# An opening in another order: C loaded by heads, the table load ahead of ScalarE's DMA issues, two weight pieces decoded in other steps (Mamba-2 SSD, then a hard-swish MLP, one core)

## The chip, the cores and the metric

The kernel runs on one core of a Trainium2 chip. The metric is the device time of one execution in microseconds (us). Three runs of the kernel before took 360.72, 358.92 and 364.13 us, median 360.72 us.

## The reference, cut to what matters

Batch is 4, heads 8, sequence 768, head size 32, state size 16; the MLP has width 256 and inner width 2048. Its weights come as float64.

```python
log_a = np.log(np.clip(a, 1e-06, 1.0))
for c in range(nc):                       # chunks of the sequence
    cum = np.cumsum(la, axis=-1)
    L = np.exp(cum[:, :, :, None] - cum[:, :, None, :]) * causal
    M = np.einsum('bhin,bhjn->bhij', Cc, Bc) * L
    y = np.einsum('bhij,bhjd->bhid', M, xc) + np.einsum('bhin,bhnd->bhid', Cc, state) * np.exp(cum)[..., None]
    state = decay_full * state + np.sum(Bx, axis=2)     # Bx: B times x, decayed to the chunk's end
...
h = x @ w_in                              # x: y with the heads joined, 3072 x 256
g = h * np.clip(h + 3.0, 0.0, 6.0) / 6.0
out = g @ w_out
```

## The kernel before, in words

The sequence is cut into six chunks of 128 positions; a chunk holds all four batches, so 512 tokens. For each chunk the kernel forms the decays L, multiplies them with C times B (`scores`, `multiply`), applies them to x (`mix`), keeps the result turned as yT (`keep`), and runs the MLP on it. A chunk is worked on in two halves of 64 positions; the second half starts from a middle state `mid`.

The schedule is written by hand: each engine executes its instructions in the order in which the program lists them, and the framework adds only waits. A tile with a tag in a pool of one buffer is given to the next tile of that tag when the last reader of the earlier one is done, wherever that reader stands in the program. PSUM banks f0 to f3, y0, y1 and two called o are passed on in this way.

**Loads.** SyncE's queue (SP) issues the loads of `a`, C, x and most weight pieces; ScalarE's queue (ACT) issues the first weight piece (`load_w(0)`) and chunk 0's B, and then loads the activation table (line 146). For chunk 0 (and chunks 3 to 5, where B comes so too) C comes through `pairs_first` (lines 96 to 103): eight DMAs of 32 KB, one for each batch b and head parity h. Each fills all 128 partitions: its source is four heads by 32 groups of positions by 64 numbers, which lie together as 256 bytes.

**Weights.** A float64 weight is decoded on the core from its two 32-bit words. Four pieces of w_in and four of w_out, 1 MB each as loaded, go through a generator `decode(i)` (lines 187 to 237), and `weights(i, n)` carries out the next n of its steps. The operations of one piece are: words (L198, ScalarE, copies the top 16 bits), masks (L215 and L217, VectorE, exponent and sign), upper (L201, VectorE, the upper significand), lower (L205, VectorE, adds the low word), two ramps on the exponent, above (L221) and below (L223, both ScalarE), sign (L228, VectorE) and product (L236, VectorE, writes w_in or w_out). Three buffers hold raw pieces.

**Opening.** For chunk 0, TensorE builds exponent differences in PSUM (`diff`), ScalarE exponentiates them (`diff_exp`, L365), B is turned by TensorE and copied by ScalarE (`turn_b`, bT), C is turned by VectorE (`turn_squares`, L465, csT) and split by head parity (`part_heads`, L472, cT). `first_eto` makes the decay from the chunk's start (e_ps in bank f0, L376), by which GpSimd fades csT (`fade`, L478). `scores(0)` multiplies C and B (cb in f0 to f3, L522) and forms the state's terms (`into_state`, L534). `multiply(0)` multiplies cb into L on VectorE (four times L563), while ScalarE copies out `adds` (`take`, L550) and `mid` (L558). `turn_cum` turns the sums of the later chunks into c_ps, in bank f1, and `by_token` (L319, VectorE) reads it. `mix(0)` multiplies L with x (L588) in two halves, u = 0 and u = 1, each followed by `from_state` (L500); its second half writes bank f1 (tile y2). `keep(0)` has four copies on ScalarE (L602). `busy(n)` is n dummy products of the identity with itself, whose result nobody reads.

Then TensorE runs the first product of the MLP for chunk 0, `mlp_in(0, f)` for f = 0 to 15 (L610); four f use one piece of w_in. Its results go through `ramp` (L688, ScalarE) and `times_ramp` (L693, VectorE), which frees the bank for f + 4. Pieces 2 to 5 are decoded between them (the `weave`), and pieces 6 and 7 after them; the second product, `first_out` (L707), follows and takes a piece of w_out in each of its four rounds.

Of the kernel before, what the change touches and what calls it, by code (L numbers as in the profile page):

```python
# [8 lines left out]
FP32 = mybir.dt.float32  # L9
# [11 lines left out]
def kernel(  # L21
# [63 lines left out]
    def load_bc(c):  # L85

        sl = slice(c * P, (c + 1) * P)

        def tokens_first(src, queue=nc.sync, **where):
            t = loads.tile([P, NB * NH, N], FP32, **where)
            queue.dma_start(out=t, in_=src[:, :, sl, :].rearrange("b h s n -> s (b h) n"))
            return t

        def pairs_first(src):
            t = loads.tile([P, 2, NB, 4, N], FP32, name="pairs", tag="bc")
            for b in range(NB):
                for h in range(2):
                    nc.sync.dma_start(  # L100
                        out=t[:, h, b].rearrange("s a n -> s (a n)"),
                        in_=src[b, h:NH:2, sl, :].rearrange("h (s a) n -> h s (a n)", a=4))
            return t

        if 0 < c < TURN:
            bcs[c] = [tokens_first(C, name="C", tag="bc")]
        Bs[c] = tokens_first(B, nc.scalar if c == 0 else nc.sync, name="B")
        if c == 0:
            bcs[c] = [pairs_first(C), Bs[c]]
        elif c < TURN:  # L110
            bcs[c].append(Bs[c])
        else:
            bcs[c] = [pairs_first(C), pairs_first(B)]
# [14 lines left out]
    def load_w(i, queue=nc.sync):  # L128
# [10 lines left out]
        queue.dma_start(out=dst, in_=src)  # L139
        raws[i] = raw  # L140

    load_w(0, nc.scalar)
    load_bc(0)
    load_x(0)
    load_w(1)
    nc.scalar.preload_act_table_set("natural_log_exp_and_others")


    ident = const.tile([P, P], FP32, name="ident")
# [37 lines left out]
    def decode(i):  # L187

        n = NK * FP * P
        top = raws[i].bitcast(U16).rearrange("p (n w) -> p n w", w=4)[:, :, 3]
        lo, hi = (raws[i].rearrange("p (n w) -> p n w", w=2)[:, :, w] for w in range(2))
        s = att.tile([P, n], U16, name="ws")
        e = att.tile([P, n], U16, name="we")
        m = att.tile([P, n], U32, name="wm")
        nc.scalar.copy(out=s, in_=top)  # L198

        def significand():  # L200
            nc.vector.tensor_scalar(  # L201
                out=m, in0=hi, scalar1=0xFFFFF, scalar2=0x100000,
                op0=ALU.bitwise_and, op1=ALU.bitwise_or)
            yield
            nc.vector.scalar_tensor_tensor(  # L205
                out=m.bitcast(FP32), in0=lo, scalar=2.0 ** -32, in1=m, op0=ALU.mult,
                op1=ALU.add)
            yield

        parts_m = significand()  # L210
        if i == 0:
            next(parts_m)
            next(parts_m)
        yield
        nc.vector.tensor_scalar(  # L215
            out=e, in0=s, scalar1=0x7FF0, scalar2=None, op0=ALU.bitwise_and)
        nc.vector.tensor_scalar(  # L217
            out=s, in0=s, scalar1=0x8000, scalar2=None, op0=ALU.bitwise_and)
        next(parts_m, None)
        yield  # L220
        nc.scalar.activation(e.bitcast(BF16), e, AF.Relu, bias=bias_hi, scale=-8.0)  # L221
        yield
        nc.scalar.activation(e, e.bitcast(BF16), AF.Relu, bias=bias_lo, scale=-1.0)  # L223
        next(parts_m, None)
        if i and i + NRAW < 2 * NP:
            load_w(i + NRAW)
        yield
        nc.vector.tensor_tensor(out=e, in0=e, in1=s, op=ALU.bitwise_or)  # L228
        m, e = m.bitcast(FP32), e.bitcast(BF16)
        if i < NP:  # L230
            dst = w_in[:, :, i * FP * P:(i + 1) * FP * P]
            m, e = (t.rearrange("p (k f) -> p k f", k=NK) for t in (m, e))
        else:
            dst = w_out[:, (i - NP) * FP:(i - NP + 1) * FP, :]
            m, e = (t.rearrange("p (k f) -> p k f", k=FP) for t in (m, e))
        nc.vector.scalar_tensor_tensor(  # L236
            out=dst, in0=m, scalar=2.0 ** -20, in1=e, op0=ALU.mult, op1=ALU.mult)

    pick = const.tile([P, G], BF16, name="pick")
    less = const.tile([P, G], BF16, name="less")
# [258 lines left out]
                    rhs=csT[pair, b, HALF[a]], start=(a == 0 and b == 0), stop=True,  # L502
                    tile_position=(32 * q, d0), skip_group_check=True)

    def scores(c):

        bT, cT, _ = bTs[c]
        cbs[c] = [ps.tile([P, NB, 2, HT], FP32, name="cb", tag=f"f{q}") for q in range(NQ)]
        both = [ps_y.tile([P, 2, NB, HT], FP32, name=f"y{u}", tag=f"y{u}") for u in range(2)]
        ys[c] = {(0, u): both[u][:, 0] for u in range(2)}
        sps[c] = [both[a if c else 1 - a][:, 1] for a in range(2)]
        if c:
            from_state(c, 0)
        for b in range(NB):
            for a, rows in enumerate(HALF):
                for q in range(NQ):  # L520
                    pair = slice(32 * q, 32 * q + 32)
                    nc.tensor.matmul(  # L522
                        out=cbs[c][q][rows, b], lhsT=bT[pair, b, rows],
                        rhs=cT[pair, b, :, rows], start=(b == 0), stop=True,
                        tile_position=(32 * q, a * HT), skip_group_check=True)
        into_state(c, 0, 1)

    def into_state(c, *halves):
# [19 lines left out]
    def take(c):  # L548
        adds[c] = att.tile([P, NB, 2 * D], FP32, name="adds", bufs=1)
        nc.scalar.copy(out=adds[c], in_=sps[c][1])  # L550

    def multiply(c):

        take(c)
        mids[c] = mid = att.tile([P, NB, 2 * D], FP32, name="mid", bufs=1)
        if c == 0:
            for t in range(2):
                nc.scalar.activation(  # L558
                    mid[:, :, t * D:(t + 1) * D], sps[c][0][:, :, t * D:(t + 1) * D], AF.Copy,
                    scale=parity[:, t:t + 1])  # L560
        for q in range(NQ):
            hs = slice(2 * q, 2 * q + 2)
            nc.vector.tensor_tensor(  # L563
                out=Ls[c][:, :, hs], in0=Ls[c][:, :, hs], in1=cbs[c][q], op=ALU.mult)
            if c and q == 1:
                new_state(mid, sps[c][0], tmps[c])
# [292 lines left out]
        mask_again(0, b)  # L859
    diff(0, 0, 1)  # L860
    diff(0, 2, 3)
    weights(0, 1)
    for b in range(NB):
        diff_exp(0, b)
    first_eto()
    diff(1, 2, 3)
    weights(0, 1)
    for b in range(NB):
        ends(0, b)
    turn_b(0)  # L870
    diff(1, 0, 1)
    weights(0, 1)
    diff_exp(1, 2)
    diff_exp(1, 3)
    turn_squares(bcs[0][0], turned(0)[2])
    part_heads(0)
    fade(0, HALF[1], nc.gpsimd)
    add_up(ends_at[1])
    store_rows()
    load_w(2)  # L880
    weights(0, 1)
    scores(0)
    multiply(0)
    load_w(3)
    c_ps = ps.tile([P, NC, G], FP32, name="c_ps", tag="f1")
    turn_cum(c_ps)
    busy(1, ps.tile([P, NB * P], FP32, name="d", tag="f0"))
    weights(0, 1)
    weights(1, 1)
    by_token(c_ps)  # L890
    mix(0)
    keep(0)
    weights(1, 3)
    renew(0)
    weights(1, 1)
    load_eto(1)
# [138 lines left out]
```

## Time and profile before

| what | us |
|---|---|
| median of three runs | 360.72 |
| the profiled execution, its own time | 359.64 |
| span of its profile (first to last instruction) | 357.9 |
| of the span, before the first L610 matmul | 23.3 |
| TensorE busy, whole span | 347.9 |
| VectorE busy, whole span | 221.9 |
| ScalarE busy, whole span | 177.5 |

All shapes and numbers below come from one profiled execution. A row of the timeline gives start, duration, engine, line, operation, and what it writes from what; in brackets stand the idle time of the engine before it and what ended that. "PEld" is TensorE's loading of the stationary operand, "SPq" an issue on SyncE's queue. A duration is from start to finish; the next instruction of VectorE or ScalarE can start some 0.1 us before an instruction ends, if it does not need its result. TensorE executes a 32-bit matmul as two instructions, so the 32 products of `mlp_in` are 64 matmuls in the profile.

### The profile page before, as it was taken

The numbers are of one execution on the slowest core, as the hardware profiler recorded it, in microseconds if no ns is written. First come the engines' busy times: TensorE is split into PE (matmuls) and PEld (weight loads), VectorE is DVE, ScalarE is ACT, GpSimd is POOL, SyncE is SP. The second block draws the span as 40 slices with busy tenths as digits, with TensorE's granted clock in tenths as the row PEclk, the third lists the DMA queues.
The fourth block names the chain that finished last, engine by engine and source line by source line (L and its number), as shares of the span: only waits on it lengthen the run. The fifth ranks groups of instructions, "written<-read, shape, count | busy, mean of one in ns | idle before, by whom it ended". The sixth has DMA issues, their size and how long they took to land.

```text
span 357.9 us, 9350 instructions
## 1 busy us (share of the span) xinstructions
PE 347.9 (97%) x3936; PEld 300.0 (84%) x3936; DVE 221.9 (62%) x426; ACT 177.5 (50%) x390; POOL 137.9 (39%) x139
## 2 busy tenths in 40 slices
PE   5799999999999999999999999999999999999996
PEld 2554458888888999888999888999888999888996
DVE  6599999975887463686444687434587431588111
ACT  4678887267763730674650575560576010476100
POOL 3300000362599521099522089610068600058700
PEclk9899999999999999999999999999999999999999
DMA  8979969502924061550043560001000000000000
GB/s 166 201 277 185 266 165 127 116 4 84 155 57 60 5 136 58 81 80 2 4 113 82 74 88 2 4 2 35 26 2 1 4 3 31 29 3 0 2 29 31
DMA packets 75482, 24.97 MB, mean 70 GB/s; under 512 B 66032, under 2 KB 71824, under 8 KB 74928
## 3 DMA queue, kind: packets, MB, share of 16 engines
q1 hardware_dynamic: 71056, 23.06, 33.9%
q10 hardware_dynamic: 4384, 1.31, 1.7%
q8 instruction: 31, 0.51, 0.6%
q14 instruction: 11, 0.09, 0.1%
HBM read 21.07 MB, written 3.29 MB: 68 GB/s over the span
## 4 chain that ended last, share of the span: by engine, by line
PE 91%; DVE 3%; DMA 3%; ACT 1%; SPq 1%; issue 0%; DVEq 0%; ACTq 0%
PE ob L766 18%; PE even L652 18%; PE oa L766 18%; PE odd L652 13%; PE o L707 8%; PE h L610 8%; PE y L588 3%; PE y L500 2%; PE cb L522 2%; DMA raw<-in_moe_w_in_dram 2%; DMA pairs<-in_C_dram 1%; PE y L534 1%; SPq L100 1%; DVE odd L681 0%; DVE up L668 0%
## 5 line engine op out<-in xcount | busy, mean ns | idle before, releaser
L752 POOL TENSOR_TENSOR s<-gT 128x512 f32<-128x512 f32 x20 | 26.4, 1318 | 89.7 <-DVE gT L693 89.7
L652 PE MATMUL even<-ts,w_sum 128*128 128x256 f32 x160 | 48.2, 383 | 0.0
L667 ACT COPY even<-odd 128x512 f32<-128x512 f32 x40 | 23.0, 576 | 48.6 <-PE odd L652 46.3
L688 ACT ACTIVATE gT<-odd,half 128x512 f32<-128x512 f32 x40 | 27.5, 688 | 34.9 <-DVE odd L681 34.9
L652 PE MATMUL odd<-yT,w_in 128*128 128x256 f32 x160 | 41.1, 379 | 0.0
L766 PE MATMUL oa<-w_out,gT 128*128 128x128 f32 x320 | 38.9, 277 | 0.0
L766 PEld LDWEIGHTS oa<-w_out,gT 128*128 128x128 f32 x320 | 38.1, 192 | 0.9
L766 PE MATMUL ob<-w_out,s 128*128 128x128 f32 x320 | 37.4, 275 | 0.0
L766 PEld LDWEIGHTS ob<-w_out,s 128*128 128x128 f32 x320 | 36.5, 192 | 0.0
L652 PEld LDWEIGHTS even<-ts,w_sum 128*128 128x128 f32 x160 | 29.9, 190 | 5.3 <-ACT up L674 1.5
L693 DVE SCALAR_TENSOR_TENSOR gT<-gT,odd 128x512 f32<-128x512 f32 x40 | 27.5, 688 | 9.9 <-ACT gT L688 9.9
L652 PEld LDWEIGHTS odd<-yT,w_in 128*128 128x128 f32 x160 | 30.1, 190 | 3.9
L385 ACT ACTIVATE L<-L,cum_n 128x64 f32<-128x64 f32 x128 | 31.1, 339 | 0.0
L766 PE MATMUL ob<-t,gT 128*128 128x128 f32 x240 | 30.3, 279 | 0.0
L688 ACT ACTIVATE gT<-even,half 128x512 f32<-128x512 f32 x40 | 27.8, 695 | 4.4 <-PE even L652 4.4
L693 DVE SCALAR_TENSOR_TENSOR gT<-gT,even 128x512 f32<-128x512 f32 x40 | 27.2, 680 | 4.4 <-ACT gT L688 4.4
L766 PEld LDWEIGHTS ob<-t,gT 128*128 128x128 f32 x240 | 27.9, 192 | 1.2 <-issue 0.5
L707 PE MATMUL o<-w_out,gT 128*128 128x256 f32 x128 | 28.7, 381 | 0.0
L668 DVE COPY up<-odd 128x256 f32<-128x256 f32 x40 | 17.0, 424 | 18.6 <-ACT even L667 17.9
L610 PE MATMUL h<-yT,w_in 128*128 128x512 f32 x64 | 27.7, 594 | 0.0
L707 PEld LDWEIGHTS o<-w_out,gT 128*128 128x128 f32 x128 | 24.1, 190 | 3.7 <-issue 0.5
L563 DVE TENSOR_TENSOR L<-L,cb 128x512 f32<-128x512 f32 x24 | 15.3, 681 | 18.0 <-PE cb L522 15.5
(130 smaller groups left out, 609.8 us busy)
## 6 DMA issues: line engine op xcount, KB each, us to landing
raw<-in_moe_w_out_dram SPq DMA_DIRECT2D x4, 1024.0 KB
L<-cum_d SPq DMA_DIRECT2D x8, 512.0 KB
xt<-in_x_dram SPq DMA_DIRECT2D x6, 512.0 KB
raw<-in_moe_w_in_dram SPq DMA_DIRECT2D x3, 1024.0 KB
out_dram<-res SPq DMA_DIRECT2D x20, 128.0 KB
eto<-cum_e SPq DMA_DIRECT2D x20, 64.0 KB
B<-in_B_dram SPq DMA_DIRECT2D x5, 256.0 KB
raw<-in_moe_w_in_dram ACTq DMA_DIRECT2D x1, 1024.0 KB
```

The source lines that it names most:

```text
L385: nc.scalar.activation(Ls[c][:, b, h], Ls[c][:, b, h], AF.Exp, bias=cum_n[:, c, g:g + 1])
L563: nc.vector.tensor_tensor(out=Ls[c][:, :, hs], in0=Ls[c][:, :, hs], in1=cbs[c][q], op=ALU.mult)
L588: nc.tensor.matmul(out=ys[c][a, u][d0:d0 + D, b], lhsT=xt[rows, b * NH + h], rhs=Ls[c][rows, b, h], start=(b == 0 and a >= min(c, 1)), sto ...
L610: nc.tensor.matmul(out=h.rearrange("p r i -> p (r i)"), lhsT=w_in[:, j, f * P:(f + 1) * P], rhs=yTs[k][:, j].rearrange("p b i -> p (b i)") ...
L652: nc.tensor.matmul(out=bank[:, r], lhsT=lhsT, rhs=rhs, start=start, stop=True, skip_group_check=True)
L667: nc.scalar.copy(out=even, in_=odd[:, 1:2].to_broadcast([P, 2, 2 * P]))
L668: nc.vector.tensor_copy(out=up[:, 1], in_=odd[:, 0])
L688: nc.scalar.activation(gTs[k][:, f], h.rearrange("p r i -> p (r i)"), AF.Relu, bias=half, scale=1.0 / 6.0)
L693: nc.vector.scalar_tensor_tensor(out=g, in0=g, scalar=1.0, in1=h.rearrange("p r i -> p (r i)"), op0=ALU.min, op1=ALU.mult)
L707: nc.tensor.matmul(out=o[:, b % 2], lhsT=gTs[0][:, f, b * P:(b + 1) * P], rhs=w_out[:, f], start=(f == 0 and b % 2 == 0), stop=True, skip_ ...
L752: nc.gpsimd.tensor_tensor(out=o, in0=p_, in1=q_, op=op)
L766: nc.tensor.matmul(out=bank[:, slot], lhsT=lhs[:, j], rhs=rhs[:, j], start=(clear and j == 0), stop=True, skip_group_check=True)
```

## The change

C's (and in chunks 3 to 5 B's) eight loads are divided by head instead of by batch: a load now fills 32 partitions with all four batches of one head. The activation table is loaded before ScalarE's two DMA issues. `decode` is rewritten as named steps with an order for piece 0, one for piece 1, and one for the rest, which is the order that those had. The opening's calls stand in another order: the second running sum and the stores first, `turn_squares` and `part_heads` before the exponentials, `first_eto` after `turn_b`, the dummy product before `scores` and not before `mix`, piece 0's lower step after `multiply`, piece 1's words after `keep`, and `by_token` after `mix`, `keep` and piece 1's upper step. Two things move inside functions: `diff(1, 0, 1)` is called between the score products and `into_state`, and `take` follows the `mid` copies in chunk 0. `load_w(3)` is issued by piece 0's step `more`.

```diff
@@ -95,11 +95,11 @@
 
         def pairs_first(src):
             t = loads.tile([P, 2, NB, 4, N], FP32, name="pairs", tag="bc")
-            for b in range(NB):
+            for q in range(NQ):
                 for h in range(2):
                     nc.sync.dma_start(
-                        out=t[:, h, b].rearrange("s a n -> s (a n)"),
-                        in_=src[b, h:NH:2, sl, :].rearrange("h (s a) n -> h s (a n)", a=4))
+                        out=t[32 * q:32 * q + 32, h].rearrange("s b a n -> s b (a n)"),
+                        in_=src[:, 2 * q + h, sl, :].rearrange("b (s a) n -> s b (a n)", a=4))
             return t
 
         if 0 < c < TURN:
@@ -139,11 +139,11 @@
         queue.dma_start(out=dst, in_=src)
         raws[i] = raw
 
+    nc.scalar.preload_act_table_set("natural_log_exp_and_others")
     load_w(0, nc.scalar)
     load_bc(0)
     load_x(0)
     load_w(1)
-    nc.scalar.preload_act_table_set("natural_log_exp_and_others")
 
 
     ident = const.tile([P, P], FP32, name="ident")
@@ -195,49 +195,59 @@
         s = att.tile([P, n], U16, name="ws")
         e = att.tile([P, n], U16, name="we")
         m = att.tile([P, n], U32, name="wm")
-        nc.scalar.copy(out=s, in_=top)
-
-        def significand():
+
+        def words():
+            nc.scalar.copy(out=s, in_=top)
+
+        def masks():
+            nc.vector.tensor_scalar(
+                out=e, in0=s, scalar1=0x7FF0, scalar2=None, op0=ALU.bitwise_and)
+            nc.vector.tensor_scalar(
+                out=s, in0=s, scalar1=0x8000, scalar2=None, op0=ALU.bitwise_and)
+
+        def upper():
             nc.vector.tensor_scalar(
                 out=m, in0=hi, scalar1=0xFFFFF, scalar2=0x100000,
                 op0=ALU.bitwise_and, op1=ALU.bitwise_or)
-            yield
+
+        def lower():
             nc.vector.scalar_tensor_tensor(
                 out=m.bitcast(FP32), in0=lo, scalar=2.0 ** -32, in1=m, op0=ALU.mult,
                 op1=ALU.add)
+
+        def above():
+            nc.scalar.activation(e.bitcast(BF16), e, AF.Relu, bias=bias_hi, scale=-8.0)
+
+        def below():
+            nc.scalar.activation(e, e.bitcast(BF16), AF.Relu, bias=bias_lo, scale=-1.0)
+
+        def more():
+            if i + NRAW < 2 * NP:
+                load_w(i + NRAW)
+
+        def sign():
+            nc.vector.tensor_tensor(out=e, in0=e, in1=s, op=ALU.bitwise_or)
+
+        def product():
+            m_, e_ = m.bitcast(FP32), e.bitcast(BF16)
+            if i < NP:
+                dst = w_in[:, :, i * FP * P:(i + 1) * FP * P]
+                m_, e_ = (t.rearrange("p (k f) -> p k f", k=NK) for t in (m_, e_))
+            else:
+                dst = w_out[:, (i - NP) * FP:(i - NP + 1) * FP, :]
+                m_, e_ = (t.rearrange("p (k f) -> p k f", k=FP) for t in (m_, e_))
+            nc.vector.scalar_tensor_tensor(
+                out=dst, in0=m_, scalar=2.0 ** -20, in1=e_, op0=ALU.mult, op1=ALU.mult)
+
+        order = {
+            0: ((words,), (masks,), (upper,), (above,), (below,), (lower,), (more,),
+                (sign, product)),
+            1: ((words,), (upper,), (masks, above), (lower, below, more), (sign, product)),
+        }.get(i, ((words,), (masks, upper), (above,), (below, lower, more), (sign, product)))
+        for step in order:
+            for part in step:
+                part()
             yield
-
-        parts_m = significand()
-        if i == 0:
-            next(parts_m)
-            next(parts_m)
-        yield
-        nc.vector.tensor_scalar(
-            out=e, in0=s, scalar1=0x7FF0, scalar2=None, op0=ALU.bitwise_and)
-        nc.vector.tensor_scalar(
-            out=s, in0=s, scalar1=0x8000, scalar2=None, op0=ALU.bitwise_and)
-        next(parts_m, None)
-        yield
-        nc.scalar.activation(e.bitcast(BF16), e, AF.Relu, bias=bias_hi, scale=-8.0)
-        yield
-        nc.scalar.activation(e, e.bitcast(BF16), AF.Relu, bias=bias_lo, scale=-1.0)
-        next(parts_m, None)
-        if i and i + NRAW < 2 * NP:
-            load_w(i + NRAW)
-        yield
-        nc.vector.tensor_tensor(out=e, in0=e, in1=s, op=ALU.bitwise_or)
-        m, e = m.bitcast(FP32), e.bitcast(BF16)
-        if i < NP:
-            dst = w_in[:, :, i * FP * P:(i + 1) * FP * P]
-            m, e = (t.rearrange("p (k f) -> p k f", k=NK) for t in (m, e))
-        else:
-            dst = w_out[:, (i - NP) * FP:(i - NP + 1) * FP, :]
-            m, e = (t.rearrange("p (k f) -> p k f", k=FP) for t in (m, e))
-        nc.vector.scalar_tensor_tensor(
-            out=dst, in0=m, scalar=2.0 ** -20, in1=e, op0=ALU.mult, op1=ALU.mult)
-
-
-
 
     pick = const.tile([P, G], BF16, name="pick")
     less = const.tile([P, G], BF16, name="less")
@@ -502,7 +512,7 @@
                     rhs=csT[pair, b, HALF[a]], start=(a == 0 and b == 0), stop=True,
                     tile_position=(32 * q, d0), skip_group_check=True)
 
-    def scores(c):
+    def scores(c, then=None):
 
 
 
@@ -523,6 +533,8 @@
                         out=cbs[c][q][rows, b], lhsT=bT[pair, b, rows],
                         rhs=cT[pair, b, :, rows], start=(b == 0), stop=True,
                         tile_position=(32 * q, a * HT), skip_group_check=True)
+        if then is not None:
+            then()
         into_state(c, 0, 1)
 
     def into_state(c, *halves):
@@ -551,13 +563,15 @@
 
     def multiply(c):
 
-        take(c)
+        if c:
+            take(c)
         mids[c] = mid = att.tile([P, NB, 2 * D], FP32, name="mid", bufs=1)
         if c == 0:
             for t in range(2):
                 nc.scalar.activation(
                     mid[:, :, t * D:(t + 1) * D], sps[c][0][:, :, t * D:(t + 1) * D], AF.Copy,
                     scale=parity[:, t:t + 1])
+            take(c)
         for q in range(NQ):
             hs = slice(2 * q, 2 * q + 2)
             nc.vector.tensor_tensor(
@@ -859,38 +873,36 @@
         mask_again(0, b)
     diff(0, 0, 1)
     diff(0, 2, 3)
-    weights(0, 1)
-    for b in range(NB):
-        diff_exp(0, b)
-    first_eto()
-    diff(1, 2, 3)
-    weights(0, 1)
-    for b in range(NB):
-        ends(0, b)
-    turn_b(0)
-    diff(1, 0, 1)
-    weights(0, 1)
-    diff_exp(1, 2)
-    diff_exp(1, 3)
-    turn_squares(bcs[0][0], turned(0)[2])
-    part_heads(0)
-    fade(0, HALF[1], nc.gpsimd)
     add_up(ends_at[1])
     store_rows()
     load_w(2)
     weights(0, 1)
-    scores(0)
+    turn_squares(bcs[0][0], turned(0)[2])
+    part_heads(0)
+    for b in range(NB):
+        diff_exp(0, b)
+        ends(0, b)
+    diff(1, 2, 3)
+    turn_b(0)
+    weights(0, 2)
+    first_eto()
+    fade(0, HALF[1], nc.gpsimd)
+    weights(0, 1)
+    diff_exp(1, 2)
+    diff_exp(1, 3)
+    weights(0, 1)
+    busy(1, ps.tile([P, NB * P], FP32, name="d", tag="f0"))
+    scores(0, lambda: diff(1, 0, 1))
     multiply(0)
-    load_w(3)
+    weights(0, 2)
     c_ps = ps.tile([P, NC, G], FP32, name="c_ps", tag="f1")
     turn_cum(c_ps)
-    busy(1, ps.tile([P, NB * P], FP32, name="d", tag="f0"))
     weights(0, 1)
-    weights(1, 1)
-    by_token(c_ps)
     mix(0)
     keep(0)
-    weights(1, 3)
+    weights(1, 2)
+    by_token(c_ps)
+    weights(1, 2)
     renew(0)
     weights(1, 1)
     load_eto(1)
```

## The prediction

> **What bounds the kernel now.** I read the busy table first, then the chain of waits in order of time, then windows of busy time, last the timeline of the opening, engine by engine. The whole-span view:
>
> ```profile
> PE   5799999999999999999999999999999999999996
> PEclk9899999999999999999999999999999999999999
> ```
>
> TensorE is busy from the third slice to the last; no wait of TensorE after 23.4 us exceeds 0.5 us. The change can gain only in the opening, or lose where TensorE is now just supplied. The chain of waits, opening part (start, duration, what):
>
> ```profile
> 0.80 5.83 DMA raw<-in_moe_w_in_dram
> ...
> 7.31 1.21 SPq L100
> ...
> 8.56 4.29 DMA pairs<-in_C_dram
> ...
> 15.19 2.12 PE cb L522 x64
> ...
> 17.31 1.30 DVE L L563 x2
> ...
> 21.91 0.84 PE y L588 x52
> 22.75 0.61 PE y L500 x16
> 23.36 27.66 PE h L610 x64
> ```
>
> The first product starts at 23.36 because C lands at 12.85 (8.56 + 4.29); its turning and splitting on VectorE, cb and `multiply` follow one another. Then windows (length, busy time of TensorE, its weight loads, VectorE, ScalarE, GpSimd, then granted clock, DMA share, GB/s):
>
> ```profile
> 8.60:10.00 1.40, 1.40 (x45) 0.93 (x40) 1.37 (x3) 1.32 (x3) 0.00 (x0) 1.00 0.37 47
> 11.66:15.07 3.41, 1.10 (x35) 0.58 (x32) 2.00 (x4) 3.33 (x5) 0.95 (x3) 1.00 1.33 159
> 15.07:18.48 3.41, 3.13 (x128) 2.59 (x128) 2.26 (x3) 0.44 (x2) 1.50 (x1) 0.50 0.99 340
> 23.30:51.00 27.70, 27.70 (x68) 12.39 (x66) 25.99 (x39) 23.41 (x30) 0.00 (x0) 1.00 0.93 196
> ```
>
> Three things: while C comes alone only 0.37 of the DMA engines are busy; cb runs at clock 0.50, after a stretch with 1.10 of 3.41 us busy; and in the first product VectorE has 25.99 of 27.70 us of work. VectorE is thus a second bound, just below TensorE. Two timeline rows matter for the new order:
>
> ```profile
> 21.57 0.28 DVE L319 TENSOR_SCALAR cum_n<-c_ps 128x128 f32<-128x128 f32 x1
> ...
> 26.77 1.23 DVE L236 SCALAR_TENSOR_TENSOR w_in<-wm,we 128x1024 f32<-128x1024 f32 x1
> ```
>
> `by_token` (L319) ends at 21.86, and the chain resumes the second half of `mix` at 21.91: bank f1 changes hands there. Piece 1's product ends at 28.00.
>
> **Loads.** Eight issues stay eight, 256-byte runs stay. Now the sixth issue waits for the first raw piece (landed 6.63), and 0.61 and 1.21 us later the eighth starts at 8.56. Without the blocked part of that 1.21 the eighth starts near 6.65 + 2 x 0.61 = 7.9. To landing the nearest rows are its own 4.29 us and `a` (issued 0.80, VectorE starts on it at 3.94: 3.1 us): C lands between 11.0 and 12.2. I take 11.0, the same bytes over more engines. The row of 0.37 fits a load on few engines.
>
> The Trainium skill, "DMA: Bandwidth & Descriptors", "Why a DMA increments its semaphore by 16 and not by 1", says a load uses the largest number of engines up to 16 that divides the slowest dimension of both sides: 4 (heads) before, 16 (32 against 32) after. The same page's "Rules for kernel authors" speaks against the change: two transfers to separate partition halves serialize, use one of 128 partitions. By the second rule alone C would still land near 12.85.
>
> **Table load first.** It takes 1.28 us (1.80 to 3.08) and ScalarE's first arithmetic starts at 4.25, so on ScalarE it is free either way. Its price is what it does to the two issues behind it, from 0 (the queue issues while the engine loads) to 1.28 us later for the raw piece and B. At 1.28 words of piece 0 starts at 7.9 and not 6.66, and the exponentials start when it ends, some 9.0 for 8.46; four of them, 2.25, then end by 11.3, before bT is due. B, landing late, could hold `turn_b` by up to the same 1.28. I take 0; the range has 1.28.
>
> **Up to cb.** TensorE's differences for chunk 1, batches 2 and 3, end at 11.1 (9.89 + 1.2); `turn_b` 0.63 to 11.7; bT 0.59 to 12.3; the copy of eto, now behind bT, 0.39 to 12.7; the dummy product waits for bank f0 and takes about 1.0 (two in 1.12); cb starts at 13.7 for 15.19. C must be ready by then: 11.0 + 0.18 + 1.09 + 0.88 = 13.15, just covered; at 12.2 it adds 0.7. Masks and upper of piece 0 (0.42 + 0.43 + 0.69) fit between 13.2 and 15.0 on VectorE. The running sum (1.20) moves into VectorE's idle time while C comes, and the stores behind it still follow the loads on SP.
>
> TensorE's longest gap before cb shrinks from 2.42 to about 0.7 us, so I take the full clock: in chunk 1, at clock 1.00, 61 of these matmuls take 1.18 us against 2.01 for 64 here. cb ends at 14.9, `multiply` starts at 14.95 for 17.31: 2.35 us earlier. `diff(1, 0, 1)` (1.2) then lies under `multiply`, before `into_state`; `mid` is out by 17.6, before the first half of `mix` needs it at 18.3. Cover: VectorE's multiply. The later `take` is only read by `renew`.
>
> **Where it is given back.** VectorE from `multiply` to `by_token`: before, 17.31 to 21.86 is 2.40 (multiply) + 0.72 (sign) + 1.14 (product) + 0.28. After, lower (1.14) and piece 1's upper (0.60) stand between: 2.40 + 1.14 + 0.72 + 1.14 + 0.60 + 0.28 = 6.28, so it ends at 21.23, 0.6 earlier. The first product can start at 22.75 for 23.36.
>
> The second payment: piece 1's words was done at 20.27 (19.13 + 1.14), in ScalarE's idle time before `keep`. Now it stands behind the four copies. The last copy ended 0.42 after the first product's start (23.78), so now at 23.2; words to 24.3. VectorE's queue has masks of piece 1 right behind `by_token`: it idles from 21.2 to 24.3. From there: exponent mask 0.42, above 1.15, below 1.15 (ScalarE; lower 1.14 and `renew` 1.06 lie under it), sign 0.72, product 1.23, some 0.1 of handovers: 29.2, against 28.00. Piece 1 is 1.2 us **later** although all before it is earlier.
>
> How much of that TensorE feels is its slack. A value of f takes 27.66/16 = 1.73, so TensorE wants piece 1 at 30.28, piece 2 at 37.2 (product row ends 35.60), piece 3 at 44.1 (43.10), the first of w_out at 51.02 (50.11): slacks 2.3, 1.6, 1.0, 0.9, since VectorE needs about 7.5 us per piece for TensorE's 6.9. With VectorE 1.2 late and full, the smallest slack goes negative: 1.2 - 0.9 = 0.3; ramps queued behind piece 1's below, and banks freed by `times_ramp` only after its product, add up to 0.4. I take +0.7. The following pieces of w_out have more room.
>
> **The clock.** After the first half of `mix` (ends near 19.0) TensorE has nothing until 21.25: 2.3 us, since the dummy product no longer stands there. Before, a stretch of 3.41 us with 1.10 busy was followed by 3.41 at 0.50, one with 1.73 busy (4.83 to 8.24, before that stretch) by clock 1.00. If the new gap falls into one stretch, the first product begins at half clock: 3.41/2 = 1.7 us lost at worst, of which the waiting for VectorE hides about 0.3: +1.4. If it is cut in two, 0. I take half, +0.7.
>
> The Trainium skill, "TensorE: Matmul & The Clock Gate", Part 1, calls the window 3413 ns, free-running; so which of 0 and 1.4 an execution gets would change from run to run, by that page.
>
> **Sum.** 359.64 (profiled execution; 1.08 below the median of 360.72) + 0.7 + 0.7 = 361.0 us. No later wait changes: loads of chunks 3 to 5 have nobody waiting in TensorE's list.
>
> **Rivals.**
> - *The hold on bank f1 does not decide* (faster). If the second half of `mix` need not wait for `by_token`, it runs at 19.0, the copies end 2.6 earlier, words follows by 20.6, and piece 1's product ends about 26.6 (29.2 - 2.6): 1.4 earlier than now. TensorE then starts the product 2.8 earlier and is held by VectorE: 1.4 + about 0.5 of slack = -1.9, 357.7. For it: cb's 2.35 us are real; against: the chain row at 21.91. It decides from where `by_token` ends before 19.
> - *C is not quicker* (slower). Landing at 12.85, the split ends at 15.05 and cb, perhaps at half clock again, runs 15.1 to 17.2: everything from `multiply` on is 2.25 later than in my sum, +2.9 without a gap's clock, 362.6. For it: the rule against halves, and shares of 1.33 for DMA just then; against: 0.37 while C came alone. Its price starts where C lands after 11.5.
> - *ScalarE's issues wait for the table*: B later by up to 1.28 holds bT, +0.8 on top of the forecast, inside the range.
>
> **Numbers.** The forecast, slower by 0.7 to 2.1, has 0.58; the hold rival 0.24; late C 0.13; the table 0.05. Likeliest case alone: 360.3 to 362.8 (its ends on the profiled time and on the median). The range reaches down to the first rival, 357.7 by the profiled time and 358.8 by the median, so 358.2, and up to late C on the median, 363.4. Two per cent, 7.2 us, is what a measurement here can tell from no change; no case reaches it. I leave 0.01 for faster and 0.02 for slower, for a wait that the trace of before cannot show.
>
> **What would show it.** C's transpose before 11.5 us; cb at clock 1.00 near 13.7; `by_token` near 21; words of piece 1 after the last L602 copy with VectorE idle some 3 us before L215; L610 starting at 22 to 23 with new waits on L236. A first product before 21, or no idle time before piece 1's masks, would prove me wrong.

## The result, and the profile after

| | before | after |
|---|---|---|
| median, 20 runs each | 359.52 us (358.65 to 364.13) | 363.52 us (362.70 to 364.65) |
| ratio after to before | | 1.0097, 95% interval 1.0073 to 1.0122 |
| the profiled execution | 359.64 us | 364.10 us |
| its span | 357.9 us | 362.4 us |
| first product of the MLP (h) starts | 23.36 us | 25.71 us |
| its 64 matmuls last | 27.66 us | 30.01 us |

The kernel became slower, by less than two per cent: 4.0 us by the medians, 4.5 by the spans. The forecast was 1.4 us slower (361.0 against 359.64); the measured median lies 0.1 us above the upper end of its range. In the two profiles the 4.5 are 2.35 (h starts later) and 2.35 (h takes longer), less 0.2 that comes back further on. The intervals here and below leave out executions that count as slow, which matters for one number only (run 10's ratio is that of six of its ten); four of the twenty executions before, 363.61 to 364.13 us, are as long as those after and are in its median, and no trace of one was kept. Two questions follow: what holds up the start, when C came 1.3 us earlier, and what makes the same 64 matmuls longer.

The chain of waits of the kernel after, opening part (start, duration, what):

```profile
7.79 3.79 DMA pairs<-in_C_dram
...
11.76 1.10 DVE csT L475
...
17.85 0.27 ACT adds L562
18.12 0.04 issue
18.17 0.84 PE y L602 x52
19.01 3.08 issue
22.09 0.42 PE y L602 x2
22.50 1.04 PE y L510 x16
23.55 1.11 PE y L602 x61
24.66 1.05 PE y L510 x16
25.71 30.01 PE h L624 x64
```

L602 is now `mix`, L510 `from_state`, L624 h. TensorE stops in the middle of a run of equal matmuls, two records short of the end of `mix`'s first half, for 3.08 us, and the row says "issue": it waited for nothing that the profile shows. Nothing in the program separates the last two records from those before them: they read the same tiles and write the same bank. Both `from_state` and the second half then take longer than before (1.05 for 0.61, 1.11 for 0.84).

The windows, laid on the steps of the clock (length, busy time of TensorE, its weight loads, VectorE, ScalarE, GpSimd, granted clock, DMA share, GB/s):

```profile
16.75:20.16 3.41, 1.66 (x107) 1.29 (x96) 3.38 (x6) 1.74 (x5) 0.00 (x0) 1.00 0.81 314
20.16:23.57 3.41, 1.48 (x26) 1.20 (x34) 1.61 (x3) 0.00 (x0) 0.00 (x0) 0.50 0.90 289
23.57:26.98 3.41, 3.41 (x82) 2.61 (x83) 0.00 (x0) 1.97 (x4) 0.00 (x0) 0.50 0.07 23
26.98:30.40 3.42, 3.42 (x5) 1.35 (x5) 3.17 (x7) 2.90 (x4) 0.00 (x0) 0.50 0.01 4
```

The granted clock is 0.50 for three windows, 10.24 us. h runs 25.71 to 30.40 in them, 4.69 us at half clock: half of it, 2.35 us, is the whole of what h takes longer.

VectorE's side, from its timeline (the brackets give the idle time before a row and what ended it):

```profile
21.48 0.28 DVE L329 TENSOR_SCALAR cum_n<-c_ps 128x128 f32<-128x128 f32 x1
27.16 0.43 DVE L203 TENSOR_SCALAR we<-ws 128x1024 uint16<-128x1024 uint16 x1 [5.40 <-ACT ws L200]
30.80 1.22 DVE L239 SCALAR_TENSOR_TENSOR w_in<-wm,we 128x1024 f32<-128x1024 f32 x1
```

`by_token` ends at 21.76, piece 1's masks wait 5.4 us for its words, and its product ends at 32.02 for 28.00 before. TensorE waits for none of it: no row of its waits names the product (L239), in matmuls or in weight loads.

### The profile page after: what moved, and what is told of

Read it like the earlier page. It is cut to its first block, busy times and chain, and to the rows that moved or that the text cites. A ratio compares the mean times of both kernels' runs of the same rounds, so it can differ in the third digit from the quotient of the medians.

```text
span 362.4 us, 9349 instructions
## 1 busy us (share of the span) xinstructions
PE 351.1 (97%) x3936; PEld 301.1 (83%) x3936; DVE 223.1 (62%) x426; ACT 177.9 (49%) x390; POOL 137.8 (38%) x139
## 4 chain that ended last, share of the span: by engine, by line
PE 90%; DVE 3%; DMA 3%; ACT 2%; issue 1%; SPq 0%; DVEq 0%; ACTq 0%
PE ob L780 18%; PE even L666 18%; PE oa L780 17%; PE odd L666 13%; PE h L624 8%; PE o L721 8%; DMA pairs<-in_C_dram 3%; PE y L602 3%; PE y L510 2%; PE cb L532 1%; PE y L546 1%; DVE odd L695 0%; DVE up L682 0%; ACT even L681 0%; DVE cT L451 0%
## 5 line engine op out<-in xcount | busy, mean ns | idle before, releaser
L624 PE MATMUL h<-yT,w_in 128*128 128x512 f32 x64 | 30.1, 634 | 0.0
L413 POOL TENSOR_TENSOR tmp<-state,eto 128x256 f32<-128x256 f32 x5 | 3.3, 655 | 65.4 <-DMA eto<-cum_e 58.2
```

The source lines that it names most:

```text
L624: nc.tensor.matmul(out=h.rearrange("p r i -> p (r i)"), lhsT=w_in[:, j, f * P:(f + 1) * P], rhs=yTs[k][:, j].rearrange("p b i -> p (b i)") ...
```

## The theories

- **F, instruction fetch.** TensorE's own instructions come in blocks by a DMA queue of their own (the queue "q8 instruction": 31 packets of 16384 bytes in the execution). The profile has 7911 records of TensorE, 255 for a packet, so a block is about 256 instructions. The stop stands behind the 705th record. F says that TensorE had reached the end of what it held and its next block, queued with the loads of weights, was late.
- **H, the hold of bank f1** (the prediction's mechanism): the second half of `mix` waits for `by_token`, 21.76.
- **K, the clock**: TensorE's idle time there costs half clock behind it.
- **W, the words**: piece 1, late behind `keep`, holds VectorE and then TensorE.

What F points to: the DMA queues in two stretches, first before from 18.0 to 18.4 us, then after from 19.7 to 20.8 (queue, kind, packets, MB, share of 16 engines).

```profile
q1 hardware_dynamic: 240, 0.09, 106.3%
q8 instruction: 1, 0.02, 15.0%
```

```profile
q1 hardware_dynamic: 28, 0.10, 53.0%
q8 instruction: 1, 0.02, 5.3%
```

One instruction packet lies in each. By the trace's DMA records (the views show no packet's own start) it starts at 18.18 before, 2.6 us ahead of TensorE's coming to its place (20.76), and at 19.74 after, 0.7 us behind TensorE's stop.

## The experiments

Times are medians; each ratio is against runs of the kernel before on the same chip. The diffs are against the kernel after unless said otherwise.

**1. Piece 2's load behind `mid`** (a small store that reads `mid` holds SP's queue, then the load goes out).

```diff
     store_rows()
-    load_w(2)
     weights(0, 1)
...
     multiply(0)
+    gate = dram.tile([16, 16], FP32, name="gate")
+    nc.sync.dma_start(out=gate, in_=mids[0][:16, 0, :16])
+    load_w(2)
     weights(0, 2)
```

> The load of weight piece 2 waits behind a small store that needs `mid` (done at 17.9 us in the changed kernel), so it is not in flight while TensorE runs its score products. Theory F (fetch): in the changed kernel TensorE stood from 19.01 to 22.09 because the next 16 KB block of its instructions was fetched late, behind piece 2 (its packet started at 19.74). Here that packet starts before 18 us and the first half of mix with its from_state (L510) ends before 20 us; the second half still waits for by_token (L329) near 21.8. Time 0.5 to 2 us under the changed kernel, ratio to the kernel before 1.004 to 1.009. Rival H (only the hold on bank f1 stopped TensorE): TensorE still stops at 19.0 with 62 of 64 matmuls done, and the time stays at ratio 1.010.

361.84 us, ratio 1.0072 (1.0045 to 1.0098). The instruction packet starts at 17.46 instead of 19.74, and the stop shrinks from 3.08 to 0.98 us (18.89 to 19.87) though no instruction of TensorE was changed. TensorE's timeline of this run:

```profile
18.05 0.84 PE L602 MATMUL y<-L,xt 64*32 64x64 f32 x62 [0.60 <-ACT adds L562]
19.87 0.30 PE L602 MATMUL y<-L,xt 64*32 64x64 f32 x2 [0.98 <-issue]
20.09 1.02 PE L510 MATMUL y<-csT,mid 32*64 32x64 f32 x16
...
21.70 1.17 PE L602 MATMUL y<-L,xt 64*32 64x64 f32 x62 [0.23 <-DVE cum_n L329]
```

The first half's `from_state` ends at 21.11 and not before 20 as expected, and the second half then waits for `by_token` until 21.70, for 0.23 us. h starts at 23.91 and lasts 29.25; the clock is at half for 6.83 us (20.25 to 27.08). F fits, and H appears as soon as F's stop is short, though it is small here.

**2. 64 instructions more ahead of the place** (32 matmuls of one column).

```diff
+    for _ in range(32):
+        nc.tensor.matmul(
+            out=ds[0, 0][:, 0], lhsT=ident_h, rhs=hide, start=True, stop=True)
     for b in range(2):
         mask_again(0, b)
```

> 32 small matmuls (64 instructions of TensorE) are added before the mask products, in time that TensorE idles; their results are overwritten. F: the end of an instruction block moves 64 instructions ahead in the program, so TensorE now stops after about 30 and not 62 of the first half's matmuls (L602), until 21.5 to 22.5 us; time within 1 us of the changed kernel, ratio 1.007 to 1.013. H: the stop stays after 62 matmuls, as the same instruction of mix waits.

366.05 us, ratio 1.0185 (1.0156 to 1.0215). The chain of waits of this run:

```profile
18.41 0.45 PE y L602 x30
18.86 2.03 issue
20.89 0.84 PE y L602 x34
...
23.89 1.04 PE y L510 x14
24.93 1.61 issue
26.53 0.47 PE y L510 x2
27.00 29.34 PE h L624 x64
```

The stop moved from 62 records to 30, which with their weight loads are 64 instructions: it goes with the instruction's number, not with any operand, and is again behind the 705th record. The next block's end, the 961st record and so 256 further, which fell into h before, now falls two records short of h and stops TensorE a second time. That second stop was not expected and makes the run slower than F's figure.

**3. `by_token` right behind the transposes of the sums.**

```diff
     turn_cum(c_ps)
+    by_token(c_ps)
     weights(0, 1)
...
     weights(1, 2)
-    by_token(c_ps)
```

> by_token (L329) stands right after the turning of the sums, before piece 0's sign and product, so bank f1 is free near 19.4 us and not 21.8. F: the fetch still stops TensorE until about 22, so the first product (L624) starts within 0.5 us of 25.6 and the time stays within 1 us of the changed kernel, ratio 1.007 to 1.012. H: the second half of mix starts near 19.7, the first product 2 us or more earlier, time 2 us or more under the changed kernel, ratio under 1.005.

363.70 us, ratio 1.0124 (1.0095 to 1.0153). `by_token` runs 2.7 us earlier (18.82 for 21.48), and the stop is still 3.00 us (18.80 to 21.80), h at 25.43. H's hold, alone removed, is worth nothing.

**4. Piece 1's words ahead of `mix` and `keep`.**

```diff
     weights(0, 1)
+    weights(1, 1)
     mix(0)
     keep(0)
-    weights(1, 2)
+    weights(1, 1)
     by_token(c_ps)
```

> Piece 1's words (L200) stands before mix and keep again. Both theories: VectorE's idle time of 5.4 us before piece 1's masks shrinks below 1 us and its product ends 3 us earlier than 32.0. F: TensorE does not feel it, since the first product starts at 25.6 at half clock and wants piece 1 only near 35: ratio 1.008 to 1.012. Theory W (the late words is what the change costs, as in the prediction): 1 to 3 us under the changed kernel, ratio 1.001 to 1.007.

363.30 us, ratio 1.0121 (1.0095 to 1.0147). VectorE's idle time ahead of the masks is gone (2.67 us of it now stand ahead of the sign, L229, waiting for ScalarE), and piece 1's product ends at 30.21; the time is as before. W is not the cost here. (This profiled opening ran 1.2 us late, cb at 15.13, so its figures for the stop, 1.87 us, and for h, 25.58, aren't compared further. Its exponent differences, L358, took 1.03 us a pair up to about 10.9 us where the kernel after has 0.61 from 7.27 on: the late opening goes with the matmuls' double length there, and runs 5, 7 and 8 have it too.)

**5. Edits 1 and 3 together.**

> The changed kernel with two edits of the earlier runs at once: the third weight piece loaded late (gate on mid), and the negation of cumT (by_token) put right behind its transposes. Theory F+H (TensorE first stands for its own instruction block, then would have stood for by_token; each edit alone leaves the other): TensorE's stop stays near 1.0 us (about 18.9 to 19.9), the second half of mix follows at once instead of at 21.7, so the first product of h starts near 22.3 (21.9 to 22.9) against 23.84 with the late load alone, and the time is 359.7 to 361.0, ratio 1.002 to 1.005. If only F mattered, h would still start near 23.8 and the ratio stay at 1.007. The granted clock is expected to be half for one or two windows of 3.41 us; at one window the lower time holds.

361.84 us over ten runs from 359.66 to 362.80; ratio 1.0023 (0.9986 to 1.0061). The stop in the profiled execution is 0.70 us, and the second half follows `from_state` at once: F and H were two holds one behind the other. The trace shows it, the time does not: the median is run 1's, and the intervals of the two ratios overlap. Its opening was the late one, and h starts at 24.01, outside the range expected; half clock stays for 6.83 us.

**6. Work in the place of the stop** (two products of the identity, results unused, three calls ahead of the block's end).

```diff
+                    if (c, u, b, h) == (0, 0, 3, 1):
+                        busy(2, ps.tile([P, NB * P], FP32, name="d", tag="f2"))
```

> The changed kernel with two products of the identity (1.29 us each, results unused) added inside the first half of mix, three matmul calls before the place where TensorE stood. Theory K (what is lost behind the stop is the clock, granted at half because TensorE stood): the stop of 3.08 us falls to under 1 us since the block has landed by the time TensorE comes to it, the clock is half for at most one window instead of 10.24 us, the second half of mix takes about 2.1 us instead of 3.6, h starts at 24.3 to 25.7 and its 64 records last 27.7 to 28.5 us instead of 30.0: 359.9 to 361.6, ratio 1.002 to 1.007. If the clock is half whatever TensorE does there, h starts at 25.7 and lasts 30: 363.5 or more. If the stop is not a fetch but a wait, it stays 3 us and comes on top of the added 2.6 us: 365 or more.

362.07 us, ratio 1.0059 (1.0040 to 1.0078), 0.5 us above the range expected, with 1.98 us of useless work of TensorE added. The granted clock on the page and a row of the chain:

```profile
PEclk9999999999999999999999999999999999999999
```

```profile
19.31 1.91 PE d L500 x4
21.23 0.23 PE y L602 x2
21.45 0.64 issue
22.09 0.31 PE y L602 x6
```

The clock never falls, and TensorE comes out of the stop at 22.09 as in the kernel after (the block's packet starts at 19.75 for 19.74): the added products only filled the time in which the block was on its way. K holds. But h (L626 in runs 6 to 8, whose edit adds two lines) now waits for VectorE, for the first time in these runs (line waited for, total, times, longest):

```profile
PEld h L626 <- DVE w_in L239: 1.9, 2, 1.2
```

**7. The same with piece 1's words ahead (edit 4).**

> The run with TensorE kept busy (two products in mix, 362.07 us), and piece 1's words ahead of mix and keep in addition: one edit against that run. Theory W' (the late words cost nothing while TensorE lost more, and became the bound when TensorE no longer stood: its chain of waits ran over VectorE's weight decode, with 1.9 us of waits for piece 1's products): VectorE's idle time of 5 us ahead of the masks is gone, piece 1's second product starts near 28.5 instead of 29.5, and the time falls by 0.6 to 1.5 us, to 360.5 to 361.5, ratio 1.002 to 1.005. If the words do not bound there, the time stays at 362.

360.66 us, ratio 1.0023 (0.9998 to 1.0049), 1.4 us less than run 6. Piece 1's product starts at 27.66 for 29.52, and h lasts 27.66, as before the change. W is real, but it shows only when nothing else is later.

**8. Edits 1, 3 and 4 with one product in `mix`.**

> The changed kernel with the third weight piece loaded late (gate on mid), by_token behind cumT's transposes, piece 1's words ahead of mix, and one product of the identity (1.29 us, result unused) three calls before the end of TensorE's block. All four named causes removed at once: the block is fetched at 17.5 to 18.5, TensorE stands under 0.7 us, no window at half the clock, second half of mix follows at once, piece 1 is ready by 29. Then h starts at 22.5 to 23.9 against 23.3 before, lasts 27.7 to 28.3, and the time is 358.0 to 360.6, ratio 0.996 to 1.003, no longer slower than before. If a cause is missing from the list, the time stays at 361 or more.

358.90 us, ratio 0.9969 (0.9940 to 0.9997). No stop, no half clock:

```profile
19.32 0.79 PE y L602 x49
20.11 1.05 PE d L500 x2
21.17 0.25 PE y L602 x8
...
23.42 27.66 PE h L626 x64
```

With the four causes out, the new order is no slower than the old one.

**9. The new order without the new loads**: C by batch and the table load behind the issues, as before.

```diff
-            for q in range(NQ):
+            for b in range(NB):
...
-    nc.scalar.preload_act_table_set("natural_log_exp_and_others")
     load_w(0, nc.scalar)
...
     load_w(1)
+    nc.scalar.preload_act_table_set("natural_log_exp_and_others")
```

> The changed kernel with C loaded by batch and the table load behind the issues again, as before: only the new order of the opening is left. F: C lands about 1.2 us later, so TensorE comes to the end of its block at about 20 instead of 18.8, while the next block still lands near 20.7: stop about 1.9 us instead of 3.1 (as in the run that began 1.2 us late with the words first), h starts at 25.5 to 26.3 and the time is 363.0 to 364.2, ratio 1.010 to 1.014: the loads' new form is worth nearly nothing in the end. If the new order by itself were harmless and the loads the cause, the time would fall to 359 to 360.5.

365.54 us, ratio 1.0162 (1.0132 to 1.0192), more than expected: the stop is 3.02 us (20.34 to 23.36), since the instruction packet too came later, at 20.86. The order alone is enough for the stop.

**10. The new loads without the new order**: the kernel before, with only these two edits.

> The kernel before with C loaded by heads and the table load ahead, the order of the work as it was. Before, the squares' transposes stand on VectorE behind Exp's tiles and much else, and C landed at 12.85 just ahead of them; scores wait for cT. F: nothing is queued that was not queued before, the block that was fetched at 18.18 stays in time, no stop; scores start up to 1.0 us earlier, and h with them: 358.3 to 359.6, ratio 0.997 to 1.001. The rival that the loads carry the loss expects 361 or more, with TensorE standing in mix.

Ten runs lay between 357.90 and 365.44 us, median 361.67, and the profile is of the one at 365.44; the ratio of 0.9994 (0.9958 to 1.0029) is not built on here. No stop was expected; what the trace shows is the same stop in the old program:

```profile
18.64 0.88 PE y L588 x53
19.52 3.62 issue
23.15 0.42 PE y L588 x2
...
26.77 30.27 PE h L610 x64
```

Its block was fetched at 20.88. Only this one of the ten has a trace, so whether the others above 362 stood there too is not shown.

**11. One move of the new order in the kernel before**: the second sum, the stores and piece 2's load early (against the kernel before).

```diff
     diff(0, 2, 3)
+    add_up(ends_at[1])
+    store_rows()
+    load_w(2)
...
     fade(0, HALF[1], nc.gpsimd)
-    add_up(ends_at[1])
-    store_rows()
-    load_w(2)
```

> The kernel before with one thing of the change: add_up of the second half, store_rows and load_w(2) moved up to stand right behind the first four diff tiles (the issue of piece 2 moves from 17.05 to some 15). Theory F with its cause in the diff: before, the queues ran empty for a moment at about 18, between the end of piece 1 and the first of piece 2, and the block asked for at 17.15 landed then (18.18); with piece 2 queued behind piece 1 there is no such moment, the block lands at 20 to 21, and TensorE, which comes to its end at about 20.8, stands 0.5 to 2 us: 360.3 to 362.5, ratio 1.002 to 1.008, and the instruction packet is late in the trace. If the moment between the pieces is not what lets the block through, the block still lands near 18.2 and the time stays at 359 to 360.

360.55 us, ratio 1.0024 (0.9987 to 1.0061): the time decides nothing. The block was fetched at 18.88 and TensorE stood for 0.93 us at its place, but the 20 to 21 us that I expected did not come: in this execution piece 2 queued early did not push the block behind it. In the profiled execution cb ran at full clock (1.25 us for 2.12), which pays for the stop.

**12. Run 10 with piece 2's load behind `mid`** (the gate of edit 1, then `load_w(2)` and `load_w(3)`).

> The kernel before with C by heads, the table load ahead, and piece 2's load behind mid (gate) with piece 3's behind it, in the old order otherwise: a try at a version faster than both. With C's loads alone its times lay between 357.9 and 365.4, and the profiled one (365.4) showed a stop of 3.6 us at the same place, its block asked for at 16.2 and fetched at 20.9, while piece 2 followed piece 1 without a gap. F: with piece 2 late the block lands by 18, no stop in any run, scores earlier by 1 us than before: 357.6 to 359.2 in every run, ratio 0.994 to 0.999. If the spread has another cause it stays, with times up to 365.

358.23 us, ratio 0.9955 (0.9929 to 0.9980): twelve runs, eleven from 357.47 to 358.65 and one at 361.30, outside the range expected for every run. This is the fastest, ahead of both kernels.

```profile
7.62 3.78 DMA pairs<-in_C_dram
...
13.76 1.25 PE cb L522 x59
...
17.84 0.88 PE y L588 x53
18.72 0.44 issue
...
21.46 27.66 PE h L610 x64
```

C lands at 11.40 for 12.85 (1.45), cb takes 1.25 for 2.12 at full clock (0.87), a stop of 0.44 remains: 1.45 + 0.87 - 0.44 = 1.88, and h starts 1.90 us earlier.

**All traces side by side.** "Asked" is the time at which TensorE executed the 449th of its records, 256 ahead of the stop's place, taken here as the moment from which the block is wanted (no row shows the request itself); "piece 1" and "piece 2" are when the last packets of these loads ended; then the instruction packet, the stop, and the time from the packet's end to TensorE's going on. All from the traces' records, by my count; an em dash: no stop.

| trace | asked | piece 1 | piece 2 | packet | stop | packet's end to go on |
|---|---|---|---|---|---|---|
| before | 17.15 | 18.19 | 21.71 | 18.18 to 19.14 | — | |
| run 11 | 16.39 | 18.52 | 21.47 | 18.88 to 19.82 | 0.93 | 1.32 |
| run 2 | 15.84 | 18.50 | 21.40 | 18.61 to 19.54 | 2.03 | 1.35 |
| run 1 | 16.24 | 17.42 | 22.97 | 17.46 to 18.58 | 0.98 | 1.29 |
| run 12 | 15.20 | 16.98 | 22.19 | 16.71 to 17.59 | 0.44 | 1.57 |
| after | 16.36 | 16.84 | 20.29 | 19.74 to 20.66 | 3.08 | 1.43 |
| run 3 | 16.15 | 16.85 | 20.21 | 19.34 to 20.35 | 3.00 | 1.45 |
| run 6 | 16.46 | 17.23 | 20.51 | 19.75 to 20.75 | 0.64 | 1.34 |
| run 9 | 17.70 | 18.53 | 21.63 | 20.86 to 21.87 | 3.02 | 1.49 |
| run 10 | 16.17 | 17.16 | 20.37 | 20.88 to 21.89 | 3.62 | 1.26 |
| run 4 | 17.44 | 17.11 | 20.88 | 19.68 to 20.69 | 1.87 | 1.27 |
| run 7 | 17.48 | 16.88 | 20.24 | 19.30 to 20.33 | — | |
| run 5 | 17.52 | 17.58 | 24.04 | 18.22 to 19.40 | 0.70 | 1.47 |
| run 8 | 17.51 | 17.75 | 23.89 | 18.25 to 19.41 | — | |

Two things stand in it. Wherever TensorE stood, it went on 1.26 to 1.57 us after the packet's end (run 2's second stop: 25.18 to 26.53, 1.35): the stop follows the packet. And the packet starts near the end of a 1 MB load: of piece 1 in the upper five (from 0.27 us ahead of its last packet's end to 0.36 behind), of piece 2 in the next seven (from 1.20 ahead, run 4, to 0.51 behind, run 10). In runs 5 and 8, where piece 1 ended within 0.3 us of the asking and no other large load was under way, it started 0.70 and 0.74 us after the asking.

With 0.7 added to "asked", the kernel after comes to 17.06: piece 1 had ended at 16.84, piece 2 was moving, and by this reading the block waited for it. For run 11 it comes to 17.09, with piece 1 moving until 18.52. The line between the two groups is thin: the kernel before comes to 17.85, 0.34 ahead of piece 1's end, and has its packet early; run 10 comes to 16.87, 0.29 ahead, and has it late. Nor is 0.7 a fixed time: a block earlier, the packet started 0.03 us after the 193rd record in the kernel before (10.60 to 10.63) and 1.92 after it in the kernel after (10.37 to 12.29). That the loads decide when the packet goes out is shown by runs 1 and 12, where moving a load moved it; by what rule is not shown. The rule was read from the finished traces, and no run was made for it alone.

## Why the prediction was right and wrong

Right: the direction, the size class (within two per cent), and the order of the opening up to `mix`. The path was wrong: the forecast added 0.7 us for late words, which cost nothing here, and 0.7 for the clock, which cost more than three times that, and had no term for TensorE's longest wait. The direction does not hang on that wait alone: run 1, with most of it gone, is still 1.0072, by a start of h 0.55 us later than before and a length 1.59 more. By its steps:

- **Loads.** C was taken to land at 11.0, bounds 11.0 to 12.2; it landed at 11.58, and its transposes start at 11.76 for the 11.2 forecast, so the sign named for it (before 11.5) missed. Of the 1.27 us against before, 0.77 are the eighth issue's (7.79 for 8.56) and 0.50 the time to landing (3.79 for 4.29). The rival that C would not be quicker is out: 12.85 before. The row of 0.37 of the DMA engines busy was the right one to read. The Trainium skill's rule in "DMA: Bandwidth & Descriptors", "Why a DMA increments its semaphore by 16 and not by 1", agrees: the trace has 4 landings for each of the old loads and 16 for each of the new. From the same page's "Rules for kernel authors", which advises against transfers to separate partition halves, the prediction had 12.85, and the trace has 11.58. But that advice compares with one load on all 16 engines, which the old loads, with 4 landings, were not, so no run here tests it.
- **Table load.** Taken at 0, and 0: it ran from 0.80 to 2.08 us while the issues behind it began at 0.83 and 1.33 (0.80 and 1.28 before).
- **Up to cb.** cb was forecast at 13.7 and at full clock; it started at 13.92, 0.39 us after the dummy product, waiting for C's split, and took 1.20. `by_token` was forecast to end at 21.23 and ended at 21.76, 0.53 later, about the 0.58 by which C was late. That the later `take` is only read by `renew` was a wrong reading: `mix` waits 0.60 us for it (`adds`, L562) and starts at 18.17, still no later than the 18.3 forecast.
- **First product at 22.75: the step that failed.** It was made from the hold on bank f1 alone. h started at 25.71, and with none of the new waits on the product that were named as a sign. At 21.8 TensorE was not waiting for `by_token`; it had stood since 19.01 for its own instructions, and stood until 22.09. That stop is only 0.3 us longer than the hold would have been, so the hold was in the forecast and the stop nearly covers it. But the stop caught the end of the first half and its `from_state`, 1.46 us of work (0.42 + 1.04) which the forecast had done before the hold, and what came behind it ran at half clock, 2.16 for 1.45. So: 0.53 (`by_token` later) + 0.33 (22.09 against 21.76) + 1.46 + 0.71 = 3.03, against 25.71 - 22.75 = 2.96 measured. No term of the sum, and no rival, had the fetch of instructions.
- **The clock: right mechanism, mis-sized.** The term was 0 or 1.4 us and I took 0.7, assuming one window at most. It was three, 4.69 us of them under h, 2.35 us; run 6 filled most of the idle time and the clock stayed full, so this part is shown.
- **The words: right on VectorE, paid for nothing in this kernel.** Idle time of 3 us forecast, 5.4 found (`keep` was later); piece 1's product was forecast at 29.2 (its own terms add up to 29.1) and ended at 32.02. The +0.7 was put on a TensorE that would start at 22.75; the real one came 3 us later and never waited. With the stop filled the same words cost 1.4 us (run 6 against run 7). Run 4, on the kernel after, shows nothing.
- **The rival "the hold on bank f1 does not decide"** gave a faster kernel, because it saw one hold where there were two. Run 3 removes the hold and gains nothing; run 8 removes the hold and the late words, shortens and fills the stop, and gains 0.3 per cent over the kernel before.
- **The range.** Its upper end, 363.4, was meant as late C on the median; by the rival's own 2.9 us that is 363.6 (360.72 + 2.9). The measured 363.52 lies between the two, which is luck, since C was not late.

## What to carry to other kernels

When a denser opening brings TensorE to a given instruction earlier, its instruction stream has to be there earlier too: count the instructions, mark every 256th (here one packet of "q8 instruction" each), and see which large load is moving when that block is fetched. An "issue" gap in the middle of equal matmuls that moves when instructions are added ahead of it points to a fetch and not to a dependency; a weight load issued later can then be the cheaper one, as in runs 1 and 12. And when one hold is removed, look for the next: here the fetch, the bank, the clock and the words lay one behind the other, and in the new order only the run with all four taken out (run 8) was below the time before.

## What the runs showed of the hardware

- TensorE stood up to 3.62 us (run 10) for a block of its own instructions, whose packet started up to 4.7 us (16.17 to 20.88) after TensorE had come to within 256 instructions of that place, while 1 MB loads of another queue were moving. The Trainium skill, "Runtime: NRT & Kernel Launch", "Instruction fetch mechanics", has the blocks of 256 instructions and their own queue, which these runs agree with; it calls the crossing "mostly hidden", which at this place it is not.
- The same skill's "DMA: Bandwidth & Descriptors", "Queues, rings and completion order", says that a DMA engine goes from queue to queue packet by packet. If the block was asked for when the table assumes, it should by that have been let in within one packet of the load, and the packet started 3.4 us later in the kernel after (16.36 to 19.74). Whether the block was held or asked for later was not found.
- TensorE went on only 1.26 to 1.57 us after the block's packet had ended.
- The clock stayed at 0.50 for one more window behind one in which TensorE was busy for all of its 3.41 us (23.57 to 26.98 in the kernel after), while in the kernel before one window with 3.13 us busy at half clock (15.07 to 18.48) was enough to end it. In both the work was mostly matmuls of 32 or 64 rows; what counts as busy there stays open.
